# Column tiles of 32 for the inter-chunk products and the state update of a fused attention and two-MoE kernel

## The chip, the cores and the metric

One NeuronCore of a Trainium2 chip runs the whole program. The metric is the device time of one execution in microseconds (us), the median over the runs shown; lower is better. The engines are named as in the profile: PE is the matrix engine, PEld its weight loader, DVE the vector engine, ACT the scalar engine, POOL the GpSimd engine, SP the queue that issues the transfers.

## What is computed

Three stages follow each other: a gated linear attention, a dense feed-forward layer, and a layer of four experts. Cut to its core, the reference is:

```python
f = 1 / (1 + np.exp(-f_logit))              # (4, 8, 768, 48): batch, heads, tokens, head size
for t in range(768):
    state = f[:, :, t, :, None] * state + np.einsum('bhd,bhe->bhde', k[:, :, t], v[:, :, t])
    y[:, :, t] = np.einsum('bhd,bhde->bhe', q[:, :, t], state)
x = y.transpose(0, 2, 1, 3).reshape(3072, 384)
h = x @ w_in                                # w_in (384, 2048)
x = (h / (1 + np.exp(-1.702 * h))) @ w_out  # w_out (2048, 384)
for e in range(4):                          # w1 (4, 384, 1024), w2 (4, 1024, 384)
    out += p[:, e:e + 1] * (np.maximum(x @ w1[e], 0) @ w2[e])
```

## The kernel before

**Attention.** The sequence of each of the four batches is cut into 6 chunks of 128 tokens, 24 chunks c in all. The eight heads are held as four pairs p; a pair fills 128 partitions, 64 for each head, of which 48 are used. Four functions make up a chunk's attention. `att0` (line 326) makes the gates' running products and scales k and q by them, with scans on DVE. `att1` (line 361) transposes k on PE (line 365), copies it to `FG` (line 366, ACT), and makes the eight heads' score matrices (line 369), which are masked on DVE (line 383) or POOL (line 378). `att2` (line 391) updates the state: on line 397 it multiplies k transposed by v, one product for each head, with 64 columns of weights and 48 columns of data streamed past them; DVE adds the old state (line 407), POOL scales the sum (line 408, `s_dec`), and ACT writes it as a block diagonal into `s_bd` (line 412). `att3` (line 418) makes the chunk's output with the products of line 437, all accumulated in one PSUM bank: the inter-chunk products ("inter" below: weights from `s_bd`, the state of the chunk before, streamed data q) and the intra-chunk products ("intra": weights v, streamed data the masked scores). The output has 384 rows, 12 blocks x of 32; block x lies in quadrant x % 4 of the partitions, at columns 128 * (x // 4). The intra products are 16, each with 32 columns of weights. The inter products are eight, four of them with 64 columns and four with 32:

```python
for x, n in ((0, 2), (2, 1), (3, 1), (4, 2), (6, 2), (8, 1), (9, 1), (10, 2)):
    jobs.append((x, n, s_bd[c % 2][:, 32 * x:32 * x + 32 * n], QKF[c % 2][:, 2, x // 3]))
```

Each has 128 rows of weights and streams 128 columns. `WORK["intra_first"]` tells for each chunk whether the intra or the inter products come first. Four chunks (the first of each batch) have no inter products, and four (the last of each batch) no state update, so 20 chunks have each of them. All these products are plain float32, and in the trace each is two loads of weights and two matmuls ("two passes"); the products of the feed-forward layers are float32r with one pass each.

**The feed-forward layers.** `L1` (line 463) and `L2` (line 487) are the two products of the dense layer, `L3` (line 515) and `L4` (line 538) those of the experts. Each value is split into a high and a low part, so that a product is three; line 279 (ACT) and line 280 (DVE or POOL) make the split, on the attention's output as well.

**Order.** A hand-written list `ORDER` mixes the first 12 chunks of attention with the weights' conversion (lines 44 to 50) and steps of L1 and L2. From token block 2 on, a table puts the attention of the chunks to come between L1 and L2 steps of the present block, one chunk to four steps (`chunk_at`). Then the experts run. From this program a scheduler makes the final order on each engine, by its own estimate of times; each engine then runs its list strictly in order, and waits on semaphores.

Of the kernel before, what the change touches and what calls it, by code (L numbers as in the profile page):

```python
# [13 lines left out]

PMIN = 2.0 ** -48

# Order of the work up to the end of the first two blocks of tokens: l<c> loads a chunk, 0<c>..3<c> are
# the parts of its attention, c<i> converts a piece of the weights, L and M are the next step of the first
# and of the second product, p makes the expert weights.
ORDER = """  # L20
00 10 01 11 20 30 l2 21 31 c0 c1 l3 c2 p c3 c7 c4 02 L c5 12 L L 22 M c6 L c8 03 32 l4 M 04 c9 M
L c10 13 M L 23 c11 M M 33 l5 c12 14 L L L 05 24 c13 34 15 L l6 M 06 L 25 M L M c14 35 M L l7 M
# [2 lines left out]
210 M 310 L M l11 011 111 L 311 211 L L M M l13 l12  # L25
""".split()

# Who does what (V: VectorE, P: GpSimdE, A: ScalarE), by chunk, piece or step; the last letter holds for the rest.
WORK = {
    "gate": "VPPAAPPVVPVP",  # L30
    "k": "VPVVVVVVVVVPV",
# [167 lines left out]
def attention_moe_moe2_kernel(  # L199
# [43 lines left out]
    s_bd = [const.tile([128, DM], F32, name=f"s_bd{i}") for i in range(2)]  # L243
# [5 lines left out]
    def carve(*shape):  # L249
        n = 1  # L250
        for s in shape:
            n *= s
        a = arena[:, pos[0]:pos[0] + n]
        pos[0] += n
        if len(shape) == 2:
            a = a.rearrange("p (a b) -> p a b", b=shape[1])
        if len(shape) == 3:
            a = a.rearrange("p (a b c) -> p a b c", b=shape[1], c=shape[2])
        return a

    QKF = [carve(3, 4, 128) for _ in range(2)]
    V = [carve(4, 128) for _ in range(2)]
    FG = [carve(516) for _ in range(2)]
# [14 lines left out]
    def split(hi, lo, src, eng):  # L278
        nc.scalar.copy(out=hi, in_=src)  # L279
        eng.tensor_tensor(out=lo, in0=src, in1=hi.bitcast(F32), op=ALU.subtract)  # L280
# [24 lines left out]
    last = NB - 1  # L305
# [3 lines left out]
    def eng(kind, i):  # L309
        o = WORK[kind]  # L310
        return o[i] if i < len(o) else o[-1]
# [1 line left out]
    def engine(kind, i):  # L313
        return nc.gpsimd if eng(kind, i) == "P" else nc.vector

# [1 line left out]
    def att_load(c):  # L317
        def go():
            t = QKF[c % 2]
            for j in (slice(0, 1), slice(1, 3)):  # L320
                for r in range(2):
                    nc.sync.dma_start(out=t[64 * r:64 * r + D, j], in_=qkf[c, r, :, j])
            nc.sync.dma_start(out=V[c % 2], in_=v[c])
        return go
# [30 lines left out]
    def ab(c):  # L355
        return bank[0:3] if c == 1 else bank[5:8]

    def scores(c, g):
        return (TH[g] if c == 1 else am[g]).rearrange("p (h t) -> p h t", h=4)
# [31 lines left out]
    def att2(c):  # L391
        def go():
            if c % CPB == CPB - 1:
                return
            for h in range(8):
                p, r = h // 2, h % 2
                nc.tensor.matmul(
                    ab(c)[0][64 * r:64 * r + 64, 48 * p:48 * p + 48],
                    FG[c % 2][:, 128 * p + 64 * r:128 * p + 64 * r + 64],
                    V[c % 2][:, p, 80 * r:80 * r + 48],  # L400
                    start=True, stop=True,
                )
            u = ab(c)[0][:, 0:192].rearrange("p (a e) -> p a e", e=48)
            if c % CPB == 0:
                nc.vector.tensor_copy(out=s_sum, in_=u)
            else:
                nc.vector.tensor_tensor(out=s_sum, in0=u, in1=s_dec, op=ALU.add)
            nc.gpsimd.tensor_tensor(
                out=s_dec, in0=s_sum, in1=PC[c % 2][:, :, 127:128].to_broadcast([128, 4, 48]), op=ALU.mult
            )  # L410
            for r in range(2):
                nc.scalar.copy(
                    out=s_bd[(c + 1) % 2].rearrange("p (a r e) -> p a r e", r=2, e=48)[64 * r:64 * r + 64, :, r],
                    in_=s_dec[64 * r:64 * r + 64],
                )
        return go

    def att3(c):
        def go():
            jobs = []  # L420
            if c % CPB:
                for x, n in ((0, 2), (2, 1), (3, 1), (4, 2), (6, 2), (8, 1), (9, 1), (10, 2)):
                    jobs.append((x, n, s_bd[c % 2][:, 32 * x:32 * x + 32 * n], QKF[c % 2][:, 2, x // 3]))
            inter, jobs = jobs, []
            av = [(x, x // 3, (0, 32, 96)[x % 3], int(x % 3 == 2)) for x in range(12)]
            av += [(3 * p + 1, p, 64, 1) for p in range(4)]
            for x, p, o, r in av:
                jobs.append((x, 1, V[c % 2][:, p, o:o + 32], scores(c, r)[:, p]))
            jobs = jobs + inter if eng("intra_first", c) == "Y" else inter + jobs
            first, final = {}, {}  # L430
            for i, (x, n, _, _) in enumerate(jobs):
                for qd in range(x % 4, x % 4 + n):
                    first.setdefault(qd, i)
                    final[qd] = i
            for i, (x, n, lhsT, rhs) in enumerate(jobs):
                q0, c0 = 32 * (x % 4), 128 * (x // 4)
                nc.tensor.matmul(  # L437
                    ab(c)[1][q0:q0 + 32 * n, c0:c0 + 128], lhsT, rhs,
                    start=i in first.values(), stop=i in final.values(),
                )  # L440
            hi, lo = xs[c // 4 % 2]
            t0 = 128 * (c % 4)
            hv = hi.rearrange("p (k t) -> p k t", k=KD)[:, :, t0:t0 + 128]
            lv = lo.rearrange("p (k t) -> p k t", k=KD)[:, :, t0:t0 + 128]
            src = ab(c)[1][:, 0:KD * 128].rearrange("p (k t) -> p k t", k=KD)
            split(hv, lv, src, nc.vector)
        return go

# [1 line left out]
    pend = []  # L450
    step_n = [0]

# [45 lines left out]
                    nc.scalar.activation(out=r, in_=bank[d], func=ACTF.Copy, scale=0.5)  # L498
                nc.sync.dma_start(out=ydram[row, d], in_=r)

# [1 line left out]
    onum = [0]  # L502
    obanks = [5, 6, 7, 0, 1, 2]

# [46 lines left out]
                if u == NU - 1:  # L551
                    nc.sync.dma_start(out=out[128 * i:128 * i + 128], in_=acc[:, i])

# [1 line left out]
    if True:  # L555
        nc.vector.memset(QKF[0][:, 0], 30.0)
        nc.gpsimd.memset(QKF[0][:, 1:3], 0.0)
# [19 lines left out]
        for g in range(4):  # L577
            for (hi, lo), w in ((win[g], w_in[g]), (wout[g], w_out[g])):
                for i in range(3):
                    c0 = slice(512 * i, 512 * i + 512)  # L580
# [135 lines left out]
        while pend:  # L716
            L4()

# [1 line left out]
    bad = nc.values_load(flag, min_val=0, max_val=1, skip_runtime_bounds_check_because="a comparison gives 0 or 1")  # L720
    with tc.If(bad > 0):
        general_path(nc, tc, dram, arena, WIDE, CV, bank, ident, qkf, v, w_in, w_out, w1, w2, probs, out)
# [48 lines left out]
```

## Time and profile before

| | us |
|---|---|
| median of 3 runs (1371.52 to 1371.73) | 1371.67 |
| span of the profiled execution | 1369.6 |
| PE busy in it | 1340.7 |
| DVE, ACT, POOL busy | 610.2, 376.2, 131.9 |

The span runs from the first to the last instruction, some 2 us less than the time of a run (1371.67 - 1369.6). The attention ends at about 480 us; behind that only the dense layer's last steps and the experts are left.

### The profile page before, as it was taken

How to read it: one execution, taken by the hardware profiler on the slowest of the kernel's cores; microseconds unless marked ns; L12 is line 12 of the kernel's file. 1: busy time of each engine (PE TensorE's matmuls, PEld its weight loads, DVE VectorE, ACT ScalarE, POOL GpSimd, SP SyncE). 2: the span in 40 equal slices, each digit the busy share in tenths (PEclk: the TensorE clock that was granted, in tenths of full speed). 3: DMA queues.
4: the chain of work that ended last, by engine and by line, in shares of the span. 5: the costliest groups of instructions: out<-in, count | busy, mean ns of one | idle time of the engine just before them, and what ended most of it. 6: DMA issues, size and time to landing. Idle time of an engine off the chain costs nothing.

```text
span 1369.6 us, 18590 instructions
## 1 busy us (share of the span) xinstructions
PE 1340.7 (98%) x7817; PEld 1157.9 (85%) x7817; DVE 610.2 (45%) x971; ACT 376.2 (27%) x674; POOL 131.9 (10%) x153
## 2 busy tenths in 40 slices
PE   5999999999999999999999999999999999999998
PEld 4777877777777788899999999999999999999997
DVE  8998456645545355433322323323333323333322
ACT  4655433333333244411211211112112112111111
POOL 5554232111101011000000000000000000000000
PEclk8889999999999999999999999999999999999999
DMA  7544022212102032300100100100000000000011
GB/s 220 162 130 145 23 68 56 74 41 74 51 26 70 1 124 69 132 23 0 47 0 1 47 0 3 45 0 20 28 0 31 17 0 1 1 0 0 30 53 60
DMA packets 30573, 64.26 MB, mean 47 GB/s; under 512 B 4368, under 2 KB 7440, under 8 KB 30480
## 3 DMA queue, kind: packets, MB, share of 16 engines
q1 hardware_dynamic: 30480, 62.98, 15.0%
q8 instruction: 63, 1.03, 0.3%
q14 instruction: 30, 0.25, 0.1%
HBM read 51.95 MB, written 11.01 MB: 46 GB/s over the span
## 4 chain that ended last, share of the span: by engine, by line


## 5 line engine op out<-in xcount | busy, mean ns | idle before, releaser
L538 PE MATMUL bank<-r,g 128*128 128x384 f32 x2304 | 434.8, 337 | 0.0
L515 PE MATMUL bank<-r,r 128*128 128x512 f32 x1728 | 430.7, 393 | 0.0
L538 PEld LDWEIGHTS bank<-r,g 128*128 128x128 f32 x2304 | 409.6, 188 | 16.8
L515 PEld LDWEIGHTS bank<-r,r 128*128 128x128 f32 x1728 | 321.4, 188 | 58.7
L522 DVE SCALAR_TENSOR_TENSOR g<-bank,g 128x512 fp32r<-128x512 f32 x192 | 132.1, 688 | 364.3 <-ACT g L521 364.3
L521 ACT ACTIVATE g<-bank 128x512 fp32r<-128x512 f32 x192 | 114.6, 597 | 617.6 <-PE bank L515 617.6
L463 PE MATMUL bank<-r,r 128*128 128x512 f32 (+1 forms) x936 | 220.8, 382 | 1.0 <-ACT r L279 0.6
L487 PE MATMUL bank<-g,r 128*128 128x512 f32 (+1 forms) x936 | 217.2, 377 | 2.5 <-DVE g L280 0.9
L487 PEld LDWEIGHTS bank<-g,r 128*128 128x128 f32 x936 | 168.0, 190 | 37.0 <-DVE g L280 1.7
L463 PEld LDWEIGHTS bank<-r,r 128*128 128x128 f32 x936 | 167.0, 192 | 35.7 <-issue 1.8
L548 DVE SCALAR_TENSOR_TENSOR arena<-bank,pr,arena 128x384 f32<-128x384 f32 x168 | 95.4, 610 | 132.6 <-PE bank L538 132.6
L471 DVE SCALAR_TENSOR_TENSOR arena<-arena,bank 128x512 f32<-128x512 f32 (+1 forms) x104 | 66.0, 636 | 91.1 <-ACT arena L470 90.9
L470 ACT ACTIVATE arena<-bank 128x512 f32<-128x512 f32 (+1 forms) x104 | 58.5, 564 | 129.9 <-PE bank L463 129.7
L280 DVE TENSOR_TENSOR g<-arena,g 128x512 fp32r<-128x512 f32 (+1 forms) x96 | 66.5, 694 | 37.8 <-ACT g L279 37.5
L280 DVE TENSOR_TENSOR r<-cv,r 128x512 fp32r<-128x512 f32 x84 | 62.8, 765 | 43.6 <-ACT r L279 26.7
L279 ACT CAST g<-arena 128x512 fp32r<-128x512 f32 (+1 forms) x104 | 60.9, 588 | 76.9 <-DVE arena L471 76.9
L279 ACT CAST r<-cv 128x512 fp32r<-128x512 f32 x90 | 54.4, 619 | 75.6 <-POOL cv L50 22.3
L50 POOL TENSOR_TENSOR cv<-cv,cv 128x512 uint32<-128x512 uint32 x24 | 35.2, 1468 | 43.5 <-DVE cv L47 34.4
L437 PE MATMUL bank<-arena,s_bd 128*64 128x128 f32 (+1 forms) x320 | 37.2, 292 | 0.8 <-DVE arena L383 0.5
L437 PEld LDWEIGHTS bank<-arena,s_bd 128*64 128x64 f32 (+1 forms) x320 | 17.5, 121 | 21.2 <-issue 19.7
L348 DVE TENSOR_TENSOR_SCAN arena<-arena,ends 128x512 f32<-128x512 f32 x24 | 34.2, 1425 | 0.2
L369 PE MATMUL bank<-arena 48*128 48x128 f32 x384 | 33.3, 309 | 0.0
(70 smaller groups left out, 526.8 us busy)
## 6 DMA issues: line engine op xcount, KB each, us to landing
cv<-in_w SPq DMA_DIRECT2D x48, 256.0 KB, 2.7
arena<-in_qkf SPq DMA_DIRECT2D x48, 192.0 KB, 3.6
arena<-in_v SPq DMA_DIRECT2D x24, 256.0 KB, 3.5
wide<-in_w_in SPq DMA_DIRECT2D x12, 512.0 KB, 5.1
wide<-in_w_out SPq DMA_DIRECT2D x12, 512.0 KB, 3.9
ydram<-cv SPq DMA_DIRECT2D x24, 256.0 KB, 2.3
cv<-ydram SPq DMA_DIRECT2D x24, 256.0 KB, 3.0
arena<-in_qkf SPq DMA_DIRECT2D x48, 96.0 KB, 3.5
```

What stands on the lines that cost most here:

```text
L279: nc.scalar.copy(out=hi, in_=src)
L280: eng.tensor_tensor(out=lo, in0=src, in1=hi.bitcast(F32), op=ALU.subtract)
L437: nc.tensor.matmul(ab(c)[1][q0:q0 + 32 * n, c0:c0 + 128], lhsT, rhs, start=i in first.values(), stop=i in final.values(),)
L463: nc.tensor.matmul(h, w[:, c0:c0 + 128], x[:, 512 * k + t0:512 * k + t0 + n], start=(i == 0), stop=(i == 8),)
L470: nc.scalar.activation(out=th, in_=h, func=ACTF.Tanh, scale=0.851)
L471: nc.vector.scalar_tensor_tensor(out=gf, in0=th, scalar=1.0, in1=h, op0=ALU.add, op1=ALU.mult)
L487: nc.tensor.matmul(bank[d][:, t0:t0 + n], w[:, c0:c0 + 128], g, start=(f == f0 and s == 0 and t0 == 0), stop=(f == f1 and s == 2 and t0 + ...
L515: nc.tensor.matmul(h, w[:, c0:c0 + 128], y[:, 512 * k:512 * k + 512], start=(i == 0), stop=(i == 8),)
L521: nc.scalar.activation(out=hi, in_=h, func=ACTF.Relu)
L522: nc.vector.scalar_tensor_tensor(out=lo, in0=h, scalar=0.0, in1=hi.bitcast(F32), op0=ALU.max, op1=ALU.subtract)
L538: nc.tensor.matmul(o, h[:, 128 * t:128 * t + 128], w[:, DM * ft:DM * ft + DM], start=(ft == 0 and s == 0), stop=(ft == 3 and s == 2),)
L548: nc.vector.scalar_tensor_tensor(out=acc[:, i], in0=o, scalar=p, in1=acc[:, i], op0=ALU.mult, op1=ALU.add)
```

## The change

Both sets of mixed or 64-column products are cut into products of 32 columns. The state update becomes 16 products for each chunk, one for each half of a head's 64 rows; the inter part of `att3` becomes 12, one for each block x. The streamed data, the sums and the places of the results are the same.

```diff
-            for h in range(8):
-                p, r = h // 2, h % 2
+            for h in range(16):
+                p, qd = h // 4, h % 4
                 nc.tensor.matmul(
-                    ab(c)[0][64 * r:64 * r + 64, 48 * p:48 * p + 48],
-                    FG[c % 2][:, 128 * p + 64 * r:128 * p + 64 * r + 64],
-                    V[c % 2][:, p, 80 * r:80 * r + 48],
+                    ab(c)[0][32 * qd:32 * qd + 32, 48 * p:48 * p + 48],
+                    FG[c % 2][:, 128 * p + 32 * qd:128 * p + 32 * qd + 32],
+                    V[c % 2][:, p, 80 * (qd // 2):80 * (qd // 2) + 48],
                     start=True, stop=True,
                 )
...
-                for x, n in ((0, 2), (2, 1), (3, 1), (4, 2), (6, 2), (8, 1), (9, 1), (10, 2)):
-                    jobs.append((x, n, s_bd[c % 2][:, 32 * x:32 * x + 32 * n], QKF[c % 2][:, 2, x // 3]))
+                for x in range(12):
+                    jobs.append((x, s_bd[c % 2][:, 32 * x:32 * x + 32], QKF[c % 2][:, 2, x // 3]))
...
-            for i, (x, n, lhsT, rhs) in enumerate(jobs):
+            for i, (x, lhsT, rhs) in enumerate(jobs):
                 q0, c0 = 32 * (x % 4), 128 * (x // 4)
                 nc.tensor.matmul(
-                    ab(c)[1][q0:q0 + 32 * n, c0:c0 + 128], lhsT, rhs,
+                    ab(c)[1][q0:q0 + 32, c0:c0 + 128], lhsT, rhs,
                     start=i in first.values(), stop=i in final.values(),
                 )
```

Since the scheduler estimates anew, the order moves as well. In what follows, `bank_95` to `bank_102` are the eight PSUM banks, and the program has one line less behind the inter products, so that line 437 is 436 in the changed kernel, 463 is 462, 487 is 486.

On PE, at one of the later chunks, where eight chunks have inter, intra and state update in a row, the list before is:

```order
L487 MATMUL bank_97<-g_87,r_74 128x512
L437 MATMUL bank_101<-arena,s_bd_113 64x128
L437 MATMUL bank_101<-arena,s_bd_113 32x128 x2
L437 MATMUL bank_101<-arena,s_bd_113 64x128 x2
L437 MATMUL bank_101<-arena,s_bd_113 32x128 x2
L437 MATMUL bank_101<-arena,s_bd_113 64x128
L437 MATMUL bank_101<-arena 32x128 x16
L397 MATMUL bank_100<-arena 64x48 x8
L463 MATMUL bank_99<-r_79,r_67 128x512 x3
```

and in the changed kernel:

```order
L486 MATMUL bank_97<-g_87,r_76 128x512
L436 MATMUL bank_101<-arena,s_bd_114 32x128 x12
L436 MATMUL bank_101<-arena 32x128 x16
L397 MATMUL bank_100<-arena 32x48 x16
L462 MATMUL bank_99<-r_79,r_69 128x512 x3
```

The neighbours are the same; what was five stretches of alternating width, then one of 32 and one of 64, is 44 products of 32. From the state update of chunk 6 on, PE's list differs by such rows alone, but for two places where a single L1 or L2 product moves past its neighbours. In the part before it does not. On PE, at the state update of an early chunk, the list before is:

```order
L397 MATMUL bank_100<-arena 64x48 x3
L463 MATMUL bank_98<-r_79,r_65 128x256 x3
L463 MATMUL bank_98<-r_80,r_65 128x256 x3
L463 MATMUL bank_99<-r_79,r_65 128x256 x3
L463 MATMUL bank_99<-r_80,r_65 128x256
L463 MATMUL bank_98<-r_79,r_66 128x256 x3
L463 MATMUL bank_99<-r_80,r_65 128x256 x2
L463 MATMUL bank_99<-r_79,r_66 128x256 x3
L397 MATMUL bank_100<-arena 64x48 x5
L437 MATMUL bank_101<-arena 32x128 x16
```

and in the changed kernel:

```order
L397 MATMUL bank_100<-arena 32x48
L462 MATMUL bank_98<-r_79,r_65 128x256 x3
L462 MATMUL bank_98<-r_80,r_65 128x256 x3
L462 MATMUL bank_99<-r_79,r_65 128x256 x3
L462 MATMUL bank_98<-r_79,r_66 128x256 x3
L462 MATMUL bank_99<-r_80,r_65 128x256 x3
L462 MATMUL bank_99<-r_79,r_66 128x256 x3
L397 MATMUL bank_100<-arena 32x48 x15
L436 MATMUL bank_101<-arena 32x128 x16
```

Before, three of the eight products ran ahead of two L1 steps; now one of sixteen does. On POOL, in the later chunks, the list before is:

```order
L352 TENSOR_TENSOR arena<-arena 128x512
L408 TENSOR_TENSOR s_dec<-s_sum,arena 128x192
L337 TENSOR_SCALAR arena<-arena 128x512
L351 COPY pend_c<-arena 128x4
L352 TENSOR_TENSOR arena<-arena 128x512
```

and in the changed kernel:

```order
L352 TENSOR_TENSOR arena<-arena 128x512
L337 TENSOR_SCALAR arena<-arena 128x512
L408 TENSOR_TENSOR s_dec<-s_sum,arena 128x192
L351 COPY pend_c<-arena 128x4
L352 TENSOR_TENSOR arena<-arena 128x512
```

The state's scaling (line 408) now stands behind the next chunk's gate (line 337).

## Rows read from the trace of the kernel before

**Rows 1.** The page's busy times: us, share of the span, instructions.

```profile
span 1369.6 us, 18590 instructions
PE 1340.7 (98%) x7817; PEld 1157.9 (85%) x7817; DVE 610.2 (45%) x971; ACT 376.2 (27%) x674; POOL 131.9 (10%) x153
```

**Rows 2.** Busy time by stretch (us from the start), with granted clock and DMA.

```profile
core 0: us, PE busy (x) PEld busy (x) DVE busy (x) ACT busy (x) POOL busy (x), PEclk, DMA share, GB/s
...
34.00:137.00 103.00, 94.90 (x822) 77.88 (x823) 96.65 (x155) 62.33 (x128) 50.52 (x48) 0.90 0.49 146
137.00:480.00 343.00, 343.00 (x2422) 269.98 (x2421) 182.18 (x282) 121.85 (x219) 53.88 (x70) 1.00 0.17 48
480.00:1365.00 885.00, 882.99 (x4383) 793.65 (x4381) 303.97 (x492) 176.40 (x300) 8.00 (x6) 1.00 0.09 28
```

**Rows 3.** PE in order of time, 280 to 286 us: start, duration, instructions, count.

```profile
279.75 1.52 PE L487 MATMUL bank<-g,r 128*128 128x512 f32 x6
281.20 1.85 PE L437 MATMUL bank<-arena,s_bd 128*64 128x128 f32 x16
282.98 1.08 PE L437 MATMUL bank<-arena 128*32 128x128 f32 x32
283.99 0.67 PE L397 MATMUL bank<-arena 128*64 128x48 f32 x16
284.60 1.66 PE L463 MATMUL bank<-r,r 128*128 128x512 f32 x6
```

**Rows 4.** The weight loader in order of time, the same stretch.

```profile
281.20 0.19 PEld L437 LDWEIGHTS bank<-arena,s_bd 128*64 128x64 f32 x2 [0.35 <-issue]
281.56 0.14 PEld L437 LDWEIGHTS bank<-arena,s_bd 128*32 128x32 f32 x4 [0.17 <-issue]
281.91 0.20 PEld L437 LDWEIGHTS bank<-arena,s_bd 128*64 128x64 f32 x4 [0.20 <-issue]
282.28 0.14 PEld L437 LDWEIGHTS bank<-arena,s_bd 128*32 128x32 f32 x4 [0.17 <-issue]
282.62 0.19 PEld L437 LDWEIGHTS bank<-arena,s_bd 128*64 128x64 f32 x2 [0.20 <-issue]
282.98 0.81 PEld L437 LDWEIGHTS bank<-arena 128*32 128x32 f32 x32 [0.17 <-issue]
283.99 0.55 PEld L397 LDWEIGHTS bank<-arena 128*64 128x64 f32 x16 [0.20 <-issue]
```

**Rows 5.** PE in order of time, other arrangements (at 186, 247 and 346 us).

```profile
186.22 0.67 PE L397 MATMUL bank<-arena 128*64 128x48 f32 x16
186.72 1.81 PE L437 MATMUL bank<-arena,s_bd 128*64 128x128 f32 x16
188.47 1.08 PE L437 MATMUL bank<-arena 128*32 128x128 f32 x32
189.48 0.74 PE L463 MATMUL bank<-r,r 128*128 128x512 f32 x2
...
247.71 1.08 PE L437 MATMUL bank<-arena 128*32 128x128 f32 x32
248.72 0.67 PE L397 MATMUL bank<-arena 128*64 128x48 f32 x16
249.32 0.96 PE L463 MATMUL bank<-r,r 128*128 128x512 f32 x3
...
346.50 1.85 PE L437 MATMUL bank<-arena,s_bd 128*64 128x128 f32 x16
348.28 1.08 PE L437 MATMUL bank<-arena 128*32 128x128 f32 x32
349.29 1.88 PE L463 MATMUL bank<-r,r 128*128 128x512 f32 x7
```

**Rows 6.** All engines in the 0.1 us from 282.95 us.

```profile
282.98 0.16 PEld L437 LDWEIGHTS bank<-arena 128*32 128x32 f32 x8 [0.17 <-issue]
282.98 0.32 PE L437 MATMUL bank<-arena 128*32 128x128 f32 x4
```

**Rows 7.** PE and loader by line, 137 to 480 us: busy us, mean ns.

```profile
L437 PE MATMUL bank<-arena,s_bd 128*64 128x128 f32 x112 | 18.2, 297 | 0.0
L397 PE MATMUL bank<-arena 128*64 128x48 f32 x208 | 8.7, 226 | 0.0
...
L437 PEld LDWEIGHTS bank<-arena 128*32 128x32 f32 x512 | 13.0, 109 | 3.1 <-issue 3.1
L397 PEld LDWEIGHTS bank<-arena 128*64 128x64 f32 x208 | 7.1, 137 | 2.8 <-issue 2.7
```

**Rows 8.** Waits in 34 to 137 us: us in total, times, longest.

```profile
PE bank L365 <- DVE arena L350: 7.8, 4, 3.4
```

**Rows 9.** POOL in order of time, 280 to 305 us.

```profile
285.24 0.52 POOL L408 TENSOR_TENSOR s_dec<-s_sum,arena 128x192 f32<-128x192 f32 x1 [17.63 <-DVE s_sum L407]
285.73 0.62 POOL L337 TENSOR_SCALAR arena<-arena 128x512 f32<-128x512 f32 x1
```

More of the change, by code (lines that the diff above doesn't have):

```diff
@@ L427, in go @@
             for x, p, o, r in av:
-                jobs.append((x, 1, V[c % 2][:, p, o:o + 32], scores(c, r)[:, p]))
+                jobs.append((x, V[c % 2][:, p, o:o + 32], scores(c, r)[:, p]))
             jobs = jobs + inter if eng("intra_first", c) == "Y" else inter + jobs
             first, final = {}, {}
[L431 to L434, printed above, removed]
-            for i, (x, n, lhsT, rhs) in enumerate(jobs):
+            for i, (x, _, _) in enumerate(jobs):
+                first.setdefault(x % 4, i)
+                final[x % 4] = i
+            for i, (x, lhsT, rhs) in enumerate(jobs):
                 q0, c0 = 32 * (x % 4), 128 * (x // 4)
                 nc.tensor.matmul(
-                    ab(c)[1][q0:q0 + 32 * n, c0:c0 + 128], lhsT, rhs,
+                    ab(c)[1][q0:q0 + 32, c0:c0 + 128], lhsT, rhs,
                     start=i in first.values(), stop=i in final.values(),
```

## The prediction

> **What bounds the kernel now.** The page first: PE is busy for 1340.7 of 1369.6 us, no other engine for even half of it [rows 1]. Since an average hides stages, the second view is the busy time by stretch [rows 2]. From 137 to 480 us, where 16 of the 24 chunks' outputs are made, PE is busy for all of 343.00 us at a granted clock of 1.00 (the upper of its two levels, 2.4 GHz), DVE for 182.18 and ACT for 121.85. There the end is set by PE alone. What is taken off PE in this stretch comes off the total, for behind it, up to 1365 us, PE is busy again for 882.99 of 885.00 us and only starts earlier. From 34 to 137 us it is otherwise: DVE is busy for 96.65 of 103.00 us and PE for 94.90, at a mean clock of 0.90. PE's largest wait there is for the scaled k (line 350) before the transposes, 7.8 us in four waits [rows 8]. PE time saved there mostly turns into more of that wait.
>
> "Busy" says nothing of how well PE is used, so the third view is PE in order of time around one chunk [rows 3]. From start to start, the eight inter products take 282.98 - 281.20 = 1.78 us, the sixteen intra products 1.01 us, the eight state products 0.61 us. Sixteen narrow products that stream the same 128 columns are thus cheaper than eight partly wider ones. The loader's rows show why [rows 4]: the inter part falls into five stretches of one width, which begin at 281.20, 281.56, 281.91, 282.28, 282.62, and each takes 0.34 to 0.37 us, whether it holds two passes or four. In front of each but the first the loader stands idle for 0.17 to 0.20 us with nothing to wait for ("issue"). It isn't the change of bank or data that does it: from the 64-wide state products to the first 64-wide inter product, another bank and other weights, PE's next starts come 186.72 - 186.22 = 0.50 us after eight products, where 0.61 is the price when another width follows [rows 3, 5]. So a change of width costs, and inside one width products of different quadrants run side by side.
>
> **The price of a slot.** Call four 32-wide passes in four quadrants a slot. A two-slot stretch of 32 columns takes 0.35 us, entry and exit included [rows 4]; the intra part, 32 passes or eight slots, takes 1.01. So one slot more costs (1.01 - 0.35) / 6 = 0.11 us, and a stretch of n slots 0.35 + (n - 2) x 0.11. The loads confirm it: after the eight that go ahead at once [rows 6], the other 24 of the 0.81 us come in six fours [rows 4].
>
> **Inter products, removed and added.** Before: 16 passes in five stretches, 1.78 us. After: 12 products, 24 passes, six slots, in one width with the intra part. Inter and intra together are 14 slots, 0.35 + 12 x 0.11 = 1.67 us, in place of 349.29 - 346.50 = 2.79 [rows 5]: 1.12 us less for a chunk.
>
> **State products.** Before, 16 passes two by two: loads of 137 ns [rows 7], 16 of them in 0.55 us, so (0.55 - 0.14) / 7 = 0.059 us a pair [rows 4]. After, 32 passes four by four, again eight steps. No row shows a slot that streams 48 columns. Bounds: 0.03 us from below, since a 32-wide load is shorter than a 64-wide one (109 against 137 ns [rows 7], two of them in a pair) and eight loads with four matmuls begin within 0.07 us [rows 6]; 0.11 us from above, a slot with 128 columns. If the streamed columns set it, 48 / 128 x 0.11 = 0.04. I take 0.04, because the 128-column slot is the nearest row of the same width and the loads fit below it. The Trainium skill ("TensorE: Matmul & The Clock Gate", section "Wait — 56ns, not 53.3ns?") says that warm starts of matmuls never come closer than about 25 ns however few columns they stream. By that a slot would take 0.10; four matmuls beginning inside 0.07 us [rows 6] don't bear it out for passes in different quadrants, so it stays a rival.
>
> **The sum by arrangement, 137 to 480 us.** There 112 of the 64-wide inter passes, eight a chunk, are 14 inter parts, and 208 state passes, 16 each, are 13 updates [rows 7]. In order of time they stand so:
> - Eight times inter, intra, state in a row: 284.60 - 281.20 = 3.40 us [rows 3]. After, one stretch: 0.35 + 13 x 0.11 + 7 x 0.04 = 2.06. 8 x 1.34 = 10.7.
> - Twice state, inter, intra: 189.48 - 186.22 = 3.26 [rows 5], after also 2.06: 2 x 1.20 = 2.4.
> - Four times inter and intra: 4 x 1.12 = 4.5.
> - Twice intra and state: 249.32 - 247.71 = 1.61 [rows 5]; after 0.35 + 7 x 0.11 + 7 x 0.04 = 1.40: 0.4.
> - Once state alone, 0.60: after 0.35 + 6 x 0.04 = 0.59, nothing.
>
> Together 18.0 us. Outside this stretch six inter parts and seven updates remain, some 6 x 1.12 + 7 x 0.05 = 7 us of PE time, all ahead of 137 us where DVE is the tighter engine. From above all 7 pass, which would need DVE's idle time (103.00 - 96.65 = 6.4 us [rows 2]) to be wholly PE's doing. From below -2: the scheduler's new order there (the split of one update, swaps on DVE and POOL) can cost a wait like the longest of 3.4 us [rows 8], partly made up. I take 2.5, since the wait before the transposes shows DVE to be the later one at the points where they meet.
>
> What is moved otherwise I cost at nothing. On POOL the state's scaling now stands behind the next gate, 0.62 us [rows 9]; it had waited 17.63 us for its input, and `s_bd` is needed one chunk, over 20 us, later. Without that slack each chunk would lose up to 0.6 us. On PE nothing new is waited for: state products follow the intra ones as before. The evacuation by ACT and DVE begins up to 1.3 us sooner, with both near half idle. No transfer is added; the next chunk's loads are issued in the same place.
>
> So 18.0 + 2.5 = 20.5 us less. The sum is made on the profiled span of 1369.6; the runs' median is 1371.67, 2 us outside the span, which the change doesn't touch: 1371.67 - 20.5 = 1351.
>
> **The rivals.**
> - A slot of 48 columns costs no less than one of 128, 0.11 us. Then the 13 updates lose 13 x 7 x 0.07 = 6.4 us, and the gain is 11.6 late and some 1.5 early: 1371.67 - 13.1 = 1358.6. For it: a pair of today's state passes takes 0.059 us, 29 ns a pass, hardly less than an intra pass with 0.11 / 4 = 27 ns, as if each pass had a fixed price. Against it: the longer 64-wide load explains the pair as well, and [rows 6].
> - The early PE time passes through in full: 18.0 + 7 makes 1346.7. For it: PE is busy for 94.90 of 103.00 us there. Against it: the waits for DVE.
> - **The slower side: the instruction supply.** Up to 44 products, 88 passes, now come without a pause, and the trace shows no such run. The densest long one is intra and state, 48 passes in 1.61 us, 34 ns each; state, inter and intra, 64 passes in 3.26 us, are 51 ns each [rows 5]. If PE can't be fed faster than this over a longer run, the pace of supply decides. The five arrangements hold 8 x 88 + 2 x 88 + 4 x 56 + 2 x 48 + 32 = 1232 passes after, and took 8 x 3.40 + 2 x 3.26 + 4 x 2.79 + 2 x 1.61 + 0.60 = 48.7 us before. Above 48.7 / 1232 = 39 ns the change loses. At 34 it still gains 48.7 - 41.9 = 6.8 us, 1365; at 51 it loses 14.1, 1386. Against it: the intra part alone goes at 32 passes in 1.01 us with its entry and exit, and the state passes behind it lose no time.
> - The change doesn't do what it says: the idle 0.2 us between inter and intra stays, because it comes from another cause than the width. Then 14 x 0.24 = 3.4 us fewer, within the range.
>
> **How the numbers follow.** A measurement of this kernel can tell 0.2%, 2.7 us, from no change. The forecast, with the slot of 48 columns at 0.03 to 0.06 us and early gains of 0 to 5, has 0.60; the dear slot 0.20; the early gain in full 0.11; the supply 0.09, a third each for a pace that still gains, one near 39 ns, and one above it. The forecast is likeliest, so 1351. The range runs from 1346, the early gain in full, to 1362, the dear slot with nothing gained early and a wait of 2 us from the new order; it leaves out the supply. Faster: 0.60 + 0.20 + 0.11 + 0.03 = 0.94; same 0.03; slower 0.03.
>
> **What would show it.** In the changed profile, at a late chunk, 56 intra and inter passes in one stretch of about 1.55 us up to the state products, those in some 0.5 us more, and no idle loader between them; state slots of 0.04 us. If they stand 0.10 us apart, the first rival holds; if the fours themselves spread beyond 0.11 us late in the stretch, the supply does. From 34 to 137 us PE should be busy for less and wait more for line 350, with DVE's busy time unchanged. The prediction is wrong if the stretch from 137 us on is shortened by other than 15 to 19 us, or if PE shows new waits in it.

## The result, and the profile after

The changed kernel takes 1359.83 us (median of 4 runs, 1358.84 to 1360.38) against 1371.7 us of the kernel before (4 runs on the same chip): 0.9909 of it, interval 0.9897 to 0.9921. So it is 11.9 us faster; the forecast was 20.5 us. The profiled execution's span is 1358.3 us, against 1369.6 [rows 1], and the sums below stand on these two.

Page and windows of the changed kernel, with the columns of [rows 2]:

```profile
span 1358.3 us, 19558 instructions
PE 1319.4 (97%) x8297; PEld 1154.7 (85%) x8297; DVE 611.4 (45%) x971; ACT 375.2 (28%) x674; POOL 133.9 (10%) x153
...
34.00:137.00 103.00, 86.97 (x918) 73.93 (x916) 93.61 (x152) 60.03 (x124) 49.38 (x46) 0.87 0.47 140
137.00:480.00 343.00, 341.39 (x2814) 279.61 (x2815) 192.79 (x295) 127.71 (x230) 56.73 (x71) 1.00 0.18 51
```

PE's busy time fell by 21.3 us and the span by 11.3: 10 us of what PE gave up came back as idle time. The second window shows PE busy almost throughout, as before. The first shows it idle for 16.0 us where it had been idle for 8.1 [rows 2]. (The windows are fixed in time, so some work has moved from one to the next.)

PE in order of time, changed kernel: first one chunk with inter, intra and state in a row, to be held against [rows 3], then the arrangements of [rows 5].

```profile
280.76 0.84 PE L486 MATMUL bank<-g,r 128*128 128x512 f32 x3
281.54 0.86 PE L436 MATMUL bank<-arena,s_bd 128*32 128x128 f32 x24
282.21 1.06 PE L436 MATMUL bank<-arena 128*32 128x128 f32 x32
283.09 0.52 PE L397 MATMUL bank<-arena 128*32 128x48 f32 x32
283.54 0.73 PE L462 MATMUL bank<-r,r 128*128 128x512 f32 x2
...
192.37 0.55 PE L397 MATMUL bank<-arena 128*32 128x48 f32 x32
192.73 0.84 PE L436 MATMUL bank<-arena,s_bd 128*32 128x128 f32 x24
193.39 1.06 PE L436 MATMUL bank<-arena 128*32 128x128 f32 x32
194.38 0.96 PE L462 MATMUL bank<-r,r 128*128 128x512 f32 x3
...
249.69 1.08 PE L436 MATMUL bank<-arena 128*32 128x128 f32 x32
250.59 0.52 PE L397 MATMUL bank<-arena 128*32 128x48 f32 x32
251.04 1.19 PE L462 MATMUL bank<-r,r 128*128 128x512 f32 x4
...
342.82 0.86 PE L436 MATMUL bank<-arena,s_bd 128*32 128x128 f32 x24
343.50 1.06 PE L436 MATMUL bank<-arena 128*32 128x128 f32 x32
344.48 0.72 PE L462 MATMUL bank<-r,r 128*128 128x512 f32 x2
```

From start to start these take 2.00, 2.01, 1.35 and 1.66 us; the forecast had 2.06, 2.06, 1.40 and 1.67. The loader's rows of the first of them show the idle time in front of each change of width gone (columns of [rows 4]):

```profile
281.53 0.59 PEld L436 LDWEIGHTS bank<-arena,s_bd 128*32 128x32 f32 x24 [0.35 <-issue]
282.11 0.89 PEld L436 LDWEIGHTS bank<-arena 128*32 128x32 f32 x32
282.98 0.49 PEld L397 LDWEIGHTS bank<-arena 128*32 128x32 f32 x32
```

The span shows the gain as well. Chunk 8's state update began at 186.22 us [rows 5] and begins at 192.37 now. From there to the end it was 1369.6 - 186.22 = 1183.4 us and is 1358.3 - 192.37 = 1165.9: 17.4 us won. But it begins 6.1 us later, where the forecast had it 2.5 us earlier. That is where the difference arose: not in the late part but ahead of it, in the part where the lists differ most.

Among the waits that grew in this part is one of DVE for POOL: 0.59 us at 132.41 us before, 2.59 us at 136.20 us now. These are DVE's row before, its rows around the wait now, and PE's for the products that wait for DVE and ACT there:

```profile
132.41 0.43 DVE L46 TENSOR_SCALAR cv<-cv 128x512 uint32<-128x512 uint32 x1 [0.59 <-POOL r L280]
```

```profile
132.93 0.68 DVE L470 SCALAR_TENSOR_TENSOR arena<-arena,bank 128x512 f32<-128x512 f32 x1
136.20 0.43 DVE L46 TENSOR_SCALAR cv<-cv 128x512 uint32<-128x512 uint32 x1 [2.59 <-POOL r L280]
136.66 0.69 DVE L47 SCALAR_TENSOR_TENSOR cv<-cv,cv 128x512 uint32<-128x512 uint32 x1
137.27 0.68 DVE L280 TENSOR_TENSOR g<-arena,g 128x512 fp32r<-128x512 f32 x1
```

```profile
135.93 0.96 PE L486 MATMUL bank<-g,r 128*128 128x512 f32 x3 [0.73 <-ACT g L279]
138.01 1.65 PE L486 MATMUL bank<-g,r 128*128 128x512 f32 x6 [1.11 <-DVE g L280]
```

### The profile page after: what moved, and what is told of

It is laid out like the page before. It is cut to its first block, busy times and chain, and to the rows that moved or that the text cites. A ratio compares the mean times of both kernels' runs of the same rounds, so it can differ in the third digit from the quotient of the medians.

```text
span 1358.3 us, 19558 instructions
## 1 busy us (share of the span) xinstructions
PE 1319.4 (97%) x8297; PEld 1154.7 (85%) x8297; DVE 611.4 (45%) x971; ACT 375.2 (28%) x674; POOL 133.9 (10%) x153
## 4 chain that ended last, share of the span: by engine, by line
PE 84%; DVE 0%; DVEq 0%; issue 0%
PE bank L537 30%; PE bank L514 29%; PE bank L462 11%; PE bank L486 11%; PE bank L436 2%; PE bank L369 1%; PE bank L365 0%; PE bank L397 0%; DVE arena L547 0%; DVEq L719 0%; PE bank L688 0%
## 5 line engine op out<-in xcount | busy, mean ns | idle before, releaser
L486 PE MATMUL bank<-g,r 128*128 128x512 f32 (+1 forms) x936 | 220.4, 381 | 7.5 <-DVE g L280 2.5
L280 DVE TENSOR_TENSOR g<-arena,g 128x512 fp32r<-128x512 f32 (+1 forms) x96 | 69.4, 724 | 40.1 <-ACT g L279 39.1
L369 PEld LDWEIGHTS bank<-arena 48*128 48x128 f32 x384 | 28.9, 214 | 5.3 <-issue 4.4
L352 POOL TENSOR_TENSOR arena<-arena 128x512 f32<-128x512 f32 x22 | 29.9, 1361 | 15.1 <-DMA arena<-in_qkf 15.1
```

The costliest lines, as they stand in the source:

```text
L369: nc.tensor.matmul(ab(c)[1 + r][:, 128 * p:128 * p + 128], kt[64 * r:64 * r + D, p], qt[64 * r:64 * r + D, p], start=True, stop=True,)
L486: nc.tensor.matmul(bank[d][:, t0:t0 + n], w[:, c0:c0 + 128], g, start=(f == f0 and s == 0 and t0 == 0), stop=(f == f1 and s == 2 and t0 + ...
```

## The experiments

**Theory A (order):** the new products cost nothing anywhere; the lists that the scheduler made anew put work that other engines wait for behind waits, ahead of 137 us. **Theory B (clock):** the new products leave PE with less to do there, and the lower mean granted clock (0.87 against 0.90 in the first window) is what makes it late, whatever the order.

To test them, a function behind the last expert step gives the scheduler one more edge between each instruction of an engine and the next of a written list. The edges are meant to fix the order only, with no wait added on the chip. With the list of the kernel before it gives that kernel's order. No run holds a kernel to its own list; that the edges cost little by themselves is seen below, where the new order comes to the same point at 192.36 us with them (and the old products) and at 192.37 without.

```diff
+PIN = {"PE": "0+115 133+3 115+6 ...", "DVE": ..., "Activation": ..., "Pool": ..., "SP": ...}
+def keep_order(nc, tc):
...
+    for a, b in zip(seq, seq[1:]):
+        tc.add_manual_dep(by[e][b], by[e][a].name, info, reason="order")
...
+        keep_order(nc, tc)
```

Lines below this function have numbers higher by 76: in the kernels with the new products the state update is line 473, `att3`'s products 512, L1 538, L2 562, the split's low part 356, the conversion 122 and 123. Where an experiment keeps some products of the old width, the numbers from `att3` on are some five higher still.

### Products and order apart

`new_old_order`: the changed kernel with the lists of the kernel before (a product that became several keeps its place). `old_new_order`: the kernel before with the lists of the changed one.

```diff
 # new_old_order: products of the change
+keep_order(nc, tc)        # PIN = the lists of the kernel before
 # old_new_order: products of the kernel before
+keep_order(nc, tc)        # PIN = the lists of the changed kernel
```

> The 32-column products in every chunk, but each engine's list held to the order of the kernel before. The changed kernel lost 6.1 us up to 186 us and won 17.4 us behind it. Theory A, the loss is the scheduler's new order: the old order brings it back, 1371.7 - 17.4 less 0 to 3 us of early gain, 1351 to 1354.5. Theory B, the loss is PE's clock: a faster PE idles more ahead of 137 us, drops to the lower level for longer, and DVE waits for products at half speed whatever the order: 1358 to 1361, with a mean clock of 0.87 or lower from 34 to 137 us.

> The products of before in every chunk, each engine's list held to the order of the changed kernel. Theory A (order): 1371.7 plus 5 to 9 us, 1377 to 1381. Theory B (clock): no loss without the faster products, 1371 to 1373.

Measured, beside 1372.16 us of the kernel before on that chip:

| | old order | new order |
|---|---|---|
| old products | 1372.16 | 1377.81 (1.0043, 1.0029 to 1.0058) |
| new products | 1353.28 (0.9862, 0.9846 to 0.9879) | 1359.83, beside 1371.7 (0.9909, 0.9897 to 0.9921) |

The products give 18.9 us in the old order and 18.0 in the new one; the order costs 5.7 us with the old products and 6.5 with the new. The two add up within 1 us. PE in order of time, `new_old_order`, then `old_new_order`, at chunk 8's state update:

```profile
185.66 0.55 PE L473 MATMUL bank<-arena 128*32 128x48 f32 x32
```

```profile
192.36 0.67 PE L474 MATMUL bank<-arena 128*64 128x48 f32 x16
```

The old products in the new order come there just as late as the changed kernel (192.37), the new products in the old order no later than the kernel before (186.22). And `new_old_order`'s first window:

```profile
34.00:137.00 103.00, 88.41 (x944) 75.03 (x942) 95.72 (x156) 61.96 (x128) 50.64 (x48) 0.92 0.50 145
```

With the new products and the old order the granted clock is 0.92, not lower than before, and both times lie where Theory A had them and not Theory B. So B falls as it was put: the order costs, and the products don't. `new_old_order` beats both kernels. The four traces, parted where chunk 8's state update begins (us; the granted clock is that up to this point):

| products, order | update begins | PE busy up to it | PE idle | clock | from it to the end |
|---|---|---|---|---|---|
| old, old (the kernel before) | 186.22 | 163.95 | 22.3 | 0.92 | 1183.4 |
| old, new | 192.36 | 163.57 | 28.8 | 0.92 | 1183.6 |
| new, old | 185.66 | 156.69 | 29.0 | 0.92 | 1165.5 |
| new, new (the changed kernel) | 192.37 | 160.94 | 31.4 | 0.89 | 1165.9 |

Behind this point the products give 17.8 us in the old order and 17.7 in the new one, and the order costs 0.3 and 0.4. Ahead of it the order costs 6.1 us with the old products, all of it idle time of PE, as Theory A says. With the new products it costs 6.7 us, and of these only 2.5 are idle time: 4.3 are the same products taking longer, at the lower clock. Whether the order brought the clock down isn't shown. It differs between single traces of equal lists as well: from 34 to 60 us, ahead of the place that `place_123` (below) moves, it is 0.75 there and 0.93 in `new_old_order`.

### What the early products give

`late_old_order`: old order, new products from chunk 8 on only.

```diff
-            for h in range(16):
...
+            w = 32 if c >= 8 else 64
+            for h in range(512 // w):
...
+                blocks = [(x, 1) for x in range(12)]
+                if not (c >= 8):
+                    blocks = ((0, 2), (2, 1), (3, 1), (4, 2), (6, 2), (8, 1), (9, 1), (10, 2))
```

> The 32-column products from chunk 8 on alone, all lists in the order of before. The part up to 137 us is then the kernel before's. Both theories: 1371.7 - 17.4 = 1354.3, within 1. Against the run with the new products everywhere in the old order it gives what they do early: under A that one is 0 to 3 us faster than this, under B 4 to 7 us slower.

1355.02 us (0.9872, 0.9856 to 0.9889). Against `new_old_order` the products of the first eight chunks are worth 1355.02 - 1353.28 = 1.7 us of the 7 that PE saves there: most of it does turn into waiting, as was forecast (22.3 us idle in the kernel before, 29.0 in `new_old_order`). How much is left isn't clear of noise. `new_old_order` starts chunk 8's update only 186.22 - 185.66 = 0.6 us ahead of the kernel before; `late_old_order`, with that kernel's products and lists up to there, starts it at 187.65 us, 1.4 later than the kernel before itself, and its runs spread from 1353.51 to 1355.88.

### State update and inter products apart

`state_old_order` and `inter_old_order`: old order, and only one of the two sets cut into 32 columns. The code is that of `late_old_order` with its two conditions held at one value:

```diff
 # state_old_order: state update in 32 columns, inter products as before
+            w = 32 if True else 64
...
+                if not (False):
 # inter_old_order: inter products in 32 columns, state update as before
+            w = 32 if False else 64
...
+                if not (True):
```

> Only the state update in 32 columns, the inter products as before, lists in the order of before. With a slot of 0.045 us as the changed trace has it, ten updates behind intra products win 0.26 us each (no change of width between, cheaper slots), the others 0 to 0.12: 1371.7 - 2.8 = 1368.9 under A; with slots of 0.11 us it would be 1374 or more. Under B somewhat more than 1369, if the seven early updates let the clock drop.

> Only the inter products in 32 columns, the state update in 64, old order. Late, 14 x 1.12 = 15.7 us less than before; ahead of 137 us 0 to 1.7 less. Against the ratio of before, 1371.7 - 15.7 - 0.9 = 1355.1. With the state update alone (2.6 less) this should add up to the 18.9 of both.

1369.61 us (0.9979, 0.997 to 0.9989) against 1372.16, and 1355.95 us (0.9887, 0.987 to 0.9903) against 1371.25: 2.6 and 15.3 us. Together that is 17.9, and 18.9 with both; a difference of 1 us between runs on different chips can't be told from none (on these two the kernel before took 1372.16 and 1371.25). PE in `state_old_order`:

```profile
280.30 1.85 PE L517 MATMUL bank<-arena,s_bd 128*64 128x128 f32 x16
282.08 1.08 PE L517 MATMUL bank<-arena 128*32 128x128 f32 x32
282.98 0.52 PE L474 MATMUL bank<-arena 128*32 128x48 f32 x32
283.43 2.33 PE L543 MATMUL bank<-r,r 128*128 128x512 f32 x9
```

The inter part keeps its 1.78 us to the next start; intra and state take 1.35 us in place of 284.60 - 282.98 = 1.62 [rows 3]. Of a chunk's gain of 1.40 us the state update has a fifth, 0.27. An update that stands between products of 128 columns before and after wins 0.12 (0.60 us before, 0.48 now; rows in the next section), so somewhat more than half of the 0.27 is the change of width that no longer stands in front of it.

### Where the order costs

Three places of the lists, at about 46, 99 and 123 us, put back into the new order one at a time, all else in the old one. Ranks are positions in an engine's list as the program is written, and only DVE's part is shown (PE, ACT, POOL and SP have theirs).

```diff
 # place_46, DVE
-45 65 62 76 56 63 66+2 91 ... 78 93 79+2 90
+65 45 76 62 56 63 66+2 91 ... 78 90 79+2 93
 # place_99, DVE
-147 139 148 164 149 143 145 150+2 144 152 154 153 146 165 155 173+2 156 175 ...
+164 147 139 148 165 143 145 149 144 150+2 154 152 166 153 146 155 173+3 156 ...
 # place_123, DVE
-171 224 192 172 193 187+2 180 194 181+2 200+2
+224 171 192+2 172 187+2 194 180 200+2 181+2
```

> New products, old order, but the new order at the first place (46 to 62 us of the trace: the score products of one chunk among L2 steps on PE, weight pieces on DVE and ACT). If the 6.5 us of the new order add up from its places: 1353.3 + 1.7 to 2.0 = 1355.2, and the profile 2 us behind the old order's from 62 us on. If one place carries it all, or only their sum matters: 1353.3 here.

> New products, old order, but the new order at the second place (99 to 116 us: a weight piece ahead of a chunk's gates on DVE, with PE, ACT and POOL to match). Adding up: 1353.3 + 1.8 to 2.4 = 1355.4; otherwise 1353.3, or 1359 if this place carries all.

> New products, old order, but the new order at the third place (121 to 142 us: L1's second halves behind weight pieces on DVE and ACT, a chunk's load on SP). Adding up: 1353.3 + 2.6 = 1355.9; otherwise 1353.3, or 1359 if this place carries all.

1354.39 us (0.9869, 0.9853 to 0.9886), 1354.97 (0.9877, 0.9861 to 0.9894) and 1356.53 (0.9886, 0.9869 to 0.9902). Above the 1353.28 of `new_old_order` that is 1.1, 1.7 and 3.2 us, together 6.0 of the 6.5. The runs of one kernel spread over up to 2.5 us (`place_123`), and these three ran on another chip than `new_old_order`. `piece_ahead` below ran with them, at 1352.99 to 1353.60: `place_99` (1354.86 to 1355.24) and `place_123` (1355.55 to 1358.07) are clear of it, `place_46` (1353.08 to 1354.45) is not. Small costs in several places, then, of which the last is half.

Four more runs take single moves out of these places.

```diff
 # scores_moved (first place): PE alone, a score product (L369 of the change)
-220+2 223 226 228+2 249 224 227 251 244 246 230 248 250
+249 220+2 223 226 224 227+3 244 246 230 248 250+2
 # piece_ahead (second): a weight piece ahead of a chunk's gate and scan on DVE; its steps on ACT and POOL too
-147 139 148 164 149 143 145 150+2 144 152 154 153 146 165
+164 147 139 148 165 149 143 145 150+2 144 152 154 166 153 146
 # act_cast_ahead (third): ACT alone, a weight's cast and copy ahead of an L1 step's cast and tanh
-140+2 149 164
+149 164 140+2
 # dve_piece_ahead (third): DVE alone, a weight's conversion ahead of an L1 step's low part
-181+2 200+2
+200+2 181+2
```

> New products, old order, and of the first place only PE's moves at 46 to 52 us, where the last score product of a chunk stands behind six L2 products instead of ahead of some. If PE's list carries the first place's 1 to 1.5 us: 1354.4 to 1355; if the weight pieces on DVE and ACT do: 1353.3.

> New products, old order, but one weight piece (lines 46, 47, 280 on DVE, its steps on ACT and POOL) pulled ahead of the gates of the chunk whose transposes wait at 104 us. If this swap is what the second place costs: as place_99, 1355 to 1355.7, with the scaled k 1.4 to 2.4 us later and PE's wait before the transposes longer by as much. If the other moves of that place are: 1353.3.

> New products, old order, and of the third place one swap on ACT alone: a weight piece's cast (line 279, waits for POOL) and its next conversion step (line 45) ahead of an L1 step's cast and the next step's tanh. If these carry the third place's 3.2 us: 1355.5 to 1356.5. If the DVE moves do: 1353.3.

> New products, old order, and of the third place one swap on DVE alone: two conversion steps (lines 46 and 47, the first waits for POOL) ahead of an L1 step's low part (line 280) and the next step's product (line 471). If this carries the third place: 1355.5 to 1356.5. If the ACT swap does: 1353.3. If they only cost together, 1353.3 in both.

1353.39 us (0.9872, 0.9855 to 0.9888), 1353.33 (0.9865, 0.9848 to 0.9881), 1354.38 (0.9875, 0.9858 to 0.9891) and 1357.46 (0.9899, 0.9882 to 0.9915). The first two moves cost nothing that can be told from noise. The third is 1.1 us above `new_old_order`, within the spread. The fourth is 4.2 us above it (3.0 by the profiles), 1 us more than was expected of it at most; it costs no less than the third place as a whole, and so carries it alone. DVE in `new_old_order`, then in `dve_piece_ahead`:

```profile
130.39 0.68 DVE L356 TENSOR_TENSOR g<-arena,g 128x512 fp32r<-128x512 f32 x1
130.99 0.67 DVE L546 SCALAR_TENSOR_TENSOR arena<-arena,bank 128x512 f32<-128x512 f32 x1
132.26 0.43 DVE L122 TENSOR_SCALAR cv<-cv 128x512 uint32<-128x512 uint32 x1 [0.60 <-POOL r L356]
132.72 0.69 DVE L123 SCALAR_TENSOR_TENSOR cv<-cv,cv 128x512 uint32<-128x512 uint32 x1
```

```profile
129.24 1.47 DVE L356 TENSOR_TENSOR r<-cv,r 128x512 fp32r<-128x512 f32 x1
132.39 0.43 DVE L122 TENSOR_SCALAR cv<-cv 128x512 uint32<-128x512 uint32 x1 [1.67 <-POOL r L356]
132.85 0.69 DVE L123 SCALAR_TENSOR_TENSOR cv<-cv,cv 128x512 uint32<-128x512 uint32 x1
133.46 0.68 DVE L356 TENSOR_TENSOR g<-arena,g 128x512 fp32r<-128x512 f32 x1
134.06 0.68 DVE L546 SCALAR_TENSOR_TENSOR arena<-arena,bank 128x512 f32<-128x512 f32 x1
```

The conversion (line 122) needs a buffer that POOL's split (line 356) still reads, and can't begin before 132.3 us in either kernel. In the old order DVE does an L1 step's low part (130.39) and the next activation (130.99) while it waits. Put behind the conversion they come at 133.46 and 134.06, 3.07 us later, and PE's L2 products, which read them, wait. PE in `new_old_order`, where they run on without a wait, then in `dve_piece_ahead`:

```profile
128.71 4.24 PE L562 MATMUL bank<-g,r 128*128 128x512 f32 x18
```

```profile
129.03 2.88 PE L562 MATMUL bank<-g,r 128*128 128x512 f32 x12
134.19 1.66 PE L562 MATMUL bank<-g,r 128*128 128x512 f32 x6 [2.29 <-DVE g L356]
```

DVE's wait for POOL, 0.60 us in the old order and 1.67 here, is the one that is 2.59 us at 136.20 us in the changed kernel, shown above. In the second place the scaled k comes later to the transposes; this is PE's wait in `new_old_order` and in `place_99`:

```profile
106.31 0.65 PE L441 MATMUL bank<-ident,arena 128*128 128x128 f32 x4 [2.14 <-DVE arena L426]
```

```profile
108.62 0.87 PE L441 MATMUL bank<-ident,arena 128*128 128x128 f32 x4 [3.70 <-DVE arena L426]
```

The weight piece ahead of the gate, first suspected of it, costs nothing by itself (`piece_ahead`). Which move of this place it is, and which of the first, stays open; the remaining moves of both places weren't tried one by one.

## Why the prediction was right, and where not

- **The late part was right, and by its mechanism.** 18.0 us were forecast; 17.4 were measured in the trace, and 17.7 and 17.8 between the traces of one order. By the starts above the arrangements give 8 x 1.40 + 2 x 1.25 + 4 x 1.13 + 2 x 0.26 + 0.12 = 18.9 us (the lone update takes 0.48; the forecast had 0.59). 0.6 of the difference to 17.4 is a new wait of PE at 213 us, below; the rest stays open.
- **The slot.** 14 slots with 128 columns take 283.09 - 281.54 = 1.55 us, 0.11 each, as read from [rows 4]. Eight state slots take 192.73 - 192.37 = 0.36 us, 0.045 each; 0.04 was taken. The dear slot at 0.11 falls, though its 1358.6 us lies nearer to the result than the forecast: a total that fits doesn't show the mechanism.
- **The idle time between the widths** was due to the width: no loader row inside the stretch waits. That rival falls.
- **The supply** falls: 88 passes in 2.00 us are 23 ns each, below the 34 ns that it had as its fastest pace.
- **POOL's swap** was rightly costed at nothing: the gate (line 337) and then the scaling (line 408) run at once when their inputs come, and behind chunk 8's update the new order costs 0.4 us in all (1165.9 against 1165.5).

```profile
284.45 0.62 POOL L337 TENSOR_SCALAR arena<-arena 128x512 f32<-128x512 f32 x1 [16.38 <-ACT arena L331]
285.03 0.51 POOL L408 TENSOR_TENSOR s_dec<-s_sum,arena 128x192 f32<-128x192 f32 x1
```

- **"If PE shows new waits":** one is new in the late part, for ACT's copy of the transposed k. By this sign, and by "on PE nothing new is waited for", the prediction was wrong, though only by 0.6 us. `new_old_order` has the wait too (0.60 us), so it comes with the products and not with the order: PE is there earlier, ACT's copy is not, for it stands behind a cast that waits for DVE (0.78 us before, 2.38 now). PE before, then PE and ACT now:

```profile
208.74 0.67 PE L397 MATMUL bank<-arena 128*64 128x48 f32 x16
209.34 2.33 PE L487 MATMUL bank<-g,r 128*128 128x512 f32 x9
```

```profile
211.33 1.16 PE L369 MATMUL bank<-arena 48*128 48x128 f32 x16
213.09 0.55 PE L397 MATMUL bank<-arena 128*32 128x48 f32 x32 [0.60 <-ACT arena L366]
213.57 0.73 PE L486 MATMUL bank<-g,r 128*128 128x512 f32 x2
```

```profile
211.93 0.62 ACT L279 CAST g<-arena 128x512 fp32r<-128x512 f32 x1 [2.38 <-DVE arena L470]
212.46 0.58 ACT L366 COPY arena<-bank 128x512 f32<-128x512 f32 x1
```

- **The step that failed is the early term, "I take 2.5".** It had two parts. The products' part was small, as forecast: 1.7 us between two kernels of one order, against 2.5, and by the traces between nothing and 2. The order's part was left at nothing, and bounded by one wait "like the longest of 3.4 us, partly made up". It was 6.5 us, in places of 1.1, 1.7 and 3.2, and little of it was made up; in the changed kernel's trace 4.3 of 6.7 us of it show as PE's products at a lower clock, for which the prediction has no term. The front showed that PE's list differs there; what decided in the one place that is settled was DVE's list, and of that the prediction only says "swaps on DVE". A reading of DVE's new list would have shown that the low part now stands behind a conversion, and [rows 2] that DVE had little slack there (96.65 of 103.00 us busy).
- "PE should wait more for line 350": it waits 7.4 us, 7.8 before [rows 8]. With the new products in the old order the sign does come, with 9.9 us. In the changed kernel about half of the new idle time is in waits for the splits (lines 279 and 280), 6.3 us in place of 2.2; `new_old_order` has 5.6 of them, so they come for the most part with the products.

So 18.0 + 1.7 - 6.5 = 13.2 us; measured were 11.9, and the runs' spread covers the rest. That the result lies inside the range is luck: the range reached up to the dear slot, which was not the cause that came.

## What to carry to other kernels

When an edit changes the number of instructions, let the lists of all engines be compared ahead of the forecast, above all where several engines are nearly full: here one DVE step put behind a wait for POOL cost 3.0 us in the trace. Measure products and order as a table of two by two; where they part, hold the old order with edges that carry no wait (here 1353.28 us, 18.9 less than before, in place of 11.9). On PE, count the changes of width and not only the products: here 32 columns throughout are more instructions and less time.

## What was not expected of the hardware

A slot of four 32-wide passes that stream 48 columns takes 0.045 us, 11 ns a pass over 32 passes. I had weighed a rule of the Trainium skill ("TensorE: Matmul & The Clock Gate", section "Wait — 56ns, not 53.3ns?") that starts come no closer than about 25 ns; by these rows it doesn't hold for passes that alternate between four quadrants. Narrower weights didn't slow the state update down: 32 passes of 32 columns take 0.48 us on their own, where 16 of 64 took 0.60.
